# Linear attention and an MLP on one core: the first two units load in runs of eight tokens

## The chip, the cores and the metric

The kernel runs on one core of one Trainium2 chip. Its engines are TensorE (PE; its weight loads stand apart as PEld), VectorE (DVE), ScalarE (ACT), GpSimd (POOL) and SyncE (SP, which here only issues transfers). All run at the same time and wait for each other by semaphores. The metric is the device time of one execution in microseconds, lower is better; before the change it is 429.2 us, the median of three runs (428.32 to 429.36).

## The reference

Two blocks stand one behind the other. The first is a gated linear attention over 4 batches, 8 heads, 768 tokens and 48 numbers per head; the second a layer norm with an MLP from 384 to 1536 channels and back, and a residual.

```python
f = 1.0 / (1.0 + np.exp(-f_logit))
for t in range(S):
    state = f[:, :, t, :, None] * state + np.einsum('bhd,bhe->bhde', k[:, :, t], v[:, :, t])
    y[:, :, t] = np.einsum('bhd,bhde->bhe', q[:, :, t], state)
x = y.transpose(0, 2, 1, 3).reshape(B, S, H * D)
xn = (x - mu) / np.sqrt(var + 1e-06) * g_ln
return x + np.maximum(xn @ w_ch1, 0.0) @ w_ch2
```

## The kernel before

The 768 tokens are cut into 12 units of 64 tokens of all 4 batches, so that a unit has 256 rows: g = 0 holds batches 0 and 1, g = 1 batches 2 and 3, 128 rows each. Attention of a unit needs f, q and k with the 48 numbers of a head on the partitions and the tokens along the free axis, while DRAM holds 48 numbers of a token in a row. So each unit's f, q and k are loaded with tokens on the partitions and turned.

`load` (L495) issues, for f, q and k of units 0 to 2, one transfer per batch: 64 partitions (tokens) by 8 heads by 48 floats, each run 192 bytes long (96 KB, 512 runs). The heads stand 64 floats apart in the buffers `fraw`, `qraw` and `kraw`, whose last 16 columns of each head are set to zero once (L416). There is one such buffer each for f, q and k, so a unit's load has to wait until the unit before has been turned. `across` (L701) turns one half g of one of the three: four 128x128 transposes on TensorE (two heads at a time) into one bank of PSUM, from which ACT takes the sigmoid (f) or DVE the product with the gates (q, k). From unit 3 on (`DIRECT`), the turning is done by transfers through DRAM: ACT splits the numbers into planes of two bytes, a transfer writes them (L473), a transposing transfer brings them back (L492). These have one buffer `turned` in common for f and q, so that q of a unit must be used up before f of the next arrives.

Then come a scan over the gates from behind (`after`, L713) and from ahead (`upto`, L724), the scores (L811), the mask (`causal`), the values (L851), the state (L889), norm and turn (L930), and the MLP: first product L948 for unit 0, L1070 for unit 1, in blocks L999 from unit 2 on; second product L1080 for unit 0, L1099 later. The weights arrive as 64-bit numbers: twelve pieces are fetched (`f`), read by ACT (`r`), clipped by DVE (`c`) and written by ACT and POOL (`w`).

Nothing reorders the work: a string, `START`, lists it word by word for the first units, and a second one, `UNIT`, for every later unit. In it `a1.k` is stage k of the attention of unit 1, `a0.k0` the same for half 0 of unit 0, `l1f` loads f of unit 1 on SP (`L`: on ACT's queue), `h00` and `m1` are steps of the MLP, `p`, `P` and `x` the plane copies and the transposing transfers, and `d` a product of the identity with itself (L621) whose result nobody reads. Each engine's queue follows the order of the list. Another string, `BANKS`, says which of four PSUM banks each use takes.

Of the kernel before, what the change touches and what calls it, by code (L numbers as in the profile page):

```python
# [300 lines left out]


BANKS = """
012302310231021300132013021301230123012301230230232012120312121213201320132031202013201320312020
132013203120201320132031202013201320312020132013203120201320132031202013201320312020132013203120
30321032
"""

PLANES = """
# [1 line left out]
"""  # L311

START = """
a0.carried l0k0 L0f1 a0.gates0 l0q0 a0.kx0 d l0k1 l0q1 a0.gates1 f a0.after0 a0.k0 a0.upto0 L0v1
a0.q0 l0v0 a0.scores0 a0.causal0 r l1f a0.after1 f c a0.upto1 d w a0.q1 a0.kx1 a0.k1 l1k f
a0.values0 a0.stats0 l1q a1.gates r a0.scores1 a1.after c a0.kt a0.causal1 d d a1.kx a0.norm0 w
a0.turn0 a1.k r a1.upto a0.chunk c a0.state h00 a0.values1 f a1.kt a1.kept f w r a1.q h00 l2f
a1.carried l1v a1.scores f f a0.stats1 a0.norm1 a1.causal c r h00 l2q a0.turn1 c w a2.gates h01 w
a1.values r a1.stats f h01 f h01 c h00 a1.chunk w r a1.norm l3f c a1.state h01 a1.turn w r h01
a2.after r c w f h00 l2k a2.kept P3f0 m1 m1 r f c w m1 a2.upto f h01 h00 c w p3f1 m0 a2.kx l3k l2v  # L320
a2.k r c m1 x3f a2.q w m0 a2.carried l4f r a2.scores p3k1 c w u a2.causal P3k0 u U a2.kt l3q l3v
a3.gates m0 m0 u a2.values P3q1 a2.chunk t u m1 u x3k u a2.stats a2.state a3.after m1 P3q0 u m0 u
l4k a2.norm u P4f1 a2.turn a3.kept u u y2 x3q a3.k m0 a3.upto m1 U p4f0 m2 m2 m2 l5f p4k1 a3.q m2
x4f P4k0 T m1 l4q m2 m2 m2 m2 p5f0 p3K0 x4k s1 m2 p4q0 P3K1 a3.kt p4q1 t a3.carried a3.scores m2
m2 m2 L5k m1 a3.causal m2 a4.gates m1 m2 P5f1 a4.after m1 x4q m2 p5k0 a4.k m1 p5k1 m1 l4v s2
a4.upto l6f m2 a4.q m2 x5f a3.chunk a3.values m2 a3.stats m2 a3.state l5v a3.norm m2 m2 P4K1 p4K0
a3.turn l5q a4.kept m2 y3 a5.gates
"""
UNIT = """
a{n}.kt a{n}.carried p{p}f1 a{o}.after a{n}.scores m{m} a{n}.causal m{m} m{m} m{m} P{o}q0 m{m}  # L330
# [8 lines left out]
def kernel(  # L339
# [19 lines left out]
    nc = tc.nc  # L359
    B, H, S, D = q.shape  # L360
    P = 128
    T = 64
    G = B // 2
    NP = H // 2
# [14 lines left out]
    HALVED = 1  # L379
    PIECE = 768  # L380
    R = 2

    outer = ctx.enter_context(tc.tile_pool(name="outer", bufs=1))
    ident = outer.tile([P, P], FP32)
# [22 lines left out]
    def one_bank(name):  # L407
        return ps1.tile([P, 512], FP32, tag=f"one{next(banks_to_use)}", name=name)
# [4 lines left out]
    wide_heads = {}  # L413
    for name in "fqk":
        t = consts.tile([P, G, H, 64], FP32, name=f"{name}raw")
        nc.gpsimd.memset(t[:, :, :, D:64], 0.0)  # L416
        wide_heads[name] = t
    loaded = {}

# [7 lines left out]
    def raw_of(n, name):  # L427

        return wide_heads["k" if n >= DIRECT and name == "q" else name]
# [3 lines left out]
    def split(n, name, i, queue):  # L433
# [28 lines left out]
        if (n, name) not in halved:  # L462
# [4 lines left out]
        src = raw_of(n, name).rearrange("p g h e -> p (g h e)")[  # L467
            :, i * D:i * D + (H - 1) * R * D + 64]
        src = bass.AP(tensor=src.tensor, offset=src.offset,
                      ap=[src.ap[0], [R * D, H], [1, 64]]).bitcast(U16).rearrange(  # L470
                          "p h (c two) -> p two h c", two=2)
# [23 lines left out]
    def load(n, name, gs=range(B // 2), engines=(nc.sync,)):  # L495
        if n >= NU:
            return
        if name != "v":
            loaded[n, name] = raw_of(n, name)
        elif (n, name) not in loaded:  # L500
            loaded[n, name] = raws.tile([P, G, H, D], FP32, tag="rawv", name=f"v{n}")
        src = {"f": f_logit, "k": k, "q": q, "v": v}[name]
        for b in (b for b in range(B) if b // 2 in gs):
            to = loaded[n, name]
            if name == "v" or n < DIRECT:
                to = to[(b % 2) * T:(b % 2 + 1) * T, b // 2, :, 0:D]
                rows = src[b, :, n * T:(n + 1) * T, :].rearrange("h p d -> p h d")
            else:
                to = to.rearrange("p g h e -> p (g h e)")[
                    b * T // R:(b + 1) * T // R, 0:H * R * D].rearrange("p (h c) -> p h c", h=H)  # L510
                rows = src[b, :, n * T:(n + 1) * T, :].rearrange("h (p i) d -> p h (i d)", i=R)
            engines[b % len(engines)].dma_start(out=to, in_=rows)  # L512

    load(0, "f", (0,), (nc.sync, nc.scalar))

    power = consts.tile([P, 2], FP32)
    nc.vector.memset(power, -0.5)
# [162 lines left out]
    def attention(n):  # L680
# [6 lines left out]
        flat = "p s e -> p (s e)"  # L687
        at = {}

        def new(name, shape, **kw):  # L690
            if name not in at:
                at[name] = work.tile(shape, FP32, tag=name, name=f"{name}{n}", **kw)
            return at[name]

        def segments(gs):
            return slice(gs[0] * HS, (gs[-1] + 1) * HS)
# [1 line left out]
        def of(gs):  # L698
            return [ega for ega in enumerate(pairs) if ega[1][0] in gs]

        def across(src, g):  # L701

            pt = one_bank(f"tr{n}")
            for a in range(NP):
                nc.tensor.transpose(pt[:, a * P:(a + 1) * P],
                                    src[:, g, 2 * a:2 * a + 2].rearrange("p h e -> p (h e)"),
                                    ident)
            return pt.rearrange("p (s t) -> p s t", t=T)
# [19 lines left out]
        def times(dst, pts, by):  # L728
            for g, pt in pts.items():
                segs = segments([g])  # L730
                nc.vector.tensor_tensor(out=dst[:, segs], in0=pt, in1=by[:, segs, 1:E1],
                                        op=ALU.mult)

        def do_gates(gs=both):
            new("after", [P, NS, E1])
            new("upto", [P, NS, E1])
            if n >= DIRECT:
                nc.scalar.activation(out=gv[:, :, 1:E1], in_=turned["f"], func=AF.Sigmoid)
                return
            for g in gs:  # L740
                pt = across(loaded[n, "f"], g)
                nc.scalar.activation(out=gv[:, segments([g]), 1:E1], in_=pt, func=AF.Sigmoid)  # L742

        def do_after(gs=both):
# [4 lines left out]

        def do_k_across(gs=both):  # L750
            if n < DIRECT:
                at.setdefault("pk", {}).update((g, across(loaded[n, "k"], g)) for g in gs)

        def do_k(gs=both):
            kh = new("kh", [P, NS, T])
# [7 lines left out]
        def do_q(gs=both):  # L763
            qh = new("qh", [P, NS, T])
            if n < DIRECT:
                times(qh, {g: across(loaded[n, "q"], g) for g in gs}, at["upto"])
            else:
                nc.vector.tensor_tensor(out=qh, in0=turned["q"], in1=at["upto"][:, :, 1:E1],
                                        op=ALU.mult)
# [476 lines left out]
```

## Time and profile before

| what | before |
|---|---|
| median of three runs | 429.2 us (428.32 to 429.36) |
| span of the profiled execution | 427.6 us |
| PE busy, share of the span | 410.9 us, 96% |
| DVE / ACT / POOL busy | 329.3 / 227.1 / 120.1 us |
| DMA packets, bytes | 157663, 68.54 MB |

The profile has no total of its own beside the span; the median of the runs stands 1.6 us above it. Times in the trace count from the start of the span. The busy time of PE counts the whole stay of a product in the pipeline, so two products that follow each other overlap in it, and a busy PE isn't a PE at its peak. In the list of instructions over time a 4-byte product of 128 rows counts as two records and a transpose as one. PEclk is the granted clock of TensorE as a share of 2.4 GHz; until its first record it is written as 1.00.

### The profile page before, as it was taken

The page shows a single profiled execution, that of the slowest core. Times are in us where ns is not written, and L with a number is a line of the kernel's source. Part 1 is how long each engine was busy: PE and PEld are TensorE (multiplying, and loading weights), DVE is VectorE, ACT ScalarE, POOL GpSimd, SP SyncE. Part 2 cuts the span into 40 slices and gives each one's busy share as a digit, 9 for nine tenths or more (in the row PEclk, how much of TensorE's full clock was granted, in tenths as well). Part 3 has the DMA queues.
Part 4 walks back from the last instruction along what each step waited for, and adds up shares of the span by engine and source line. Part 5 has one row for each costly group of instructions (what it writes and reads, how often), then busy time and mean ns, then how long its engine had stood idle before and what let it go on. Part 6 is the DMA issues. An engine that isn't in the chain of part 4 may idle for free.

```text
span 427.6 us, 13031 instructions
## 1 busy us (share of the span) xinstructions
PE 410.9 (96%) x5509; PEld 391.7 (92%) x5509; DVE 329.3 (77%) x530; ACT 227.1 (53%) x380; POOL 120.1 (28%) x162
## 2 busy tenths in 40 slices
PE   4889999999999999999999989999999999999995
PEld 3769888779999999999999989999999999999995
DVE  5784866999797978878878868878878878664561
ACT  2579988446535574574574563573583451341320
POOL 2425536315224033033034024024025022022021
PEclk9899999999999999999999999999999999999998
DMA  9999998888999878879897869789977840100001
GB/s 133 239 224 264 207 239 197 212 181 204 217 226 174 205 161 208 191 164 201 171 197 182 201 131 209 181 191 196 174 173 166 181 89 10 31 2 18 20 11 34
DMA packets 157663, 68.54 MB, mean 160 GB/s; under 512 B 144976, under 2 KB 148240, under 8 KB 157600
## 3 DMA queue, kind: packets, MB, share of 16 engines
q1 hardware_dynamic: 144144, 52.94, 60.5%
q0 software_dynamic: 3648, 11.72, 8.0%
q10 hardware_dynamic: 9808, 3.00, 3.6%
q8 instruction: 45, 0.74, 0.7%
q14 instruction: 18, 0.15, 0.1%
HBM read 28.31 MB, written 22.02 MB: 118 GB/s over the span
## 4 chain that ended last, share of the span: by engine, by line
PE 90%; DMA 5%; SPq 2%; issue 1%; DVE 1%; ACT 1%; ACTq 0%
PE pp L1099 35%; PE bx L999 12%; PE by L999 11%; PE bz L999 4%; PE ph L1070 4%; PE po L1080 4%; PE ph L948 3%; PE py L851 3%; PE py L797 3%; DMA kraw<-in_k_dram 2%; PE bw L999 2%; PE shared L811 2%; PE bv L999 2%; PE shared L889 2%; PE xp L930 2%; SPq L512 2%
## 5 line engine op out<-in xcount | busy, mean ns | idle before, releaser
L1010 ACT ACTIVATE h<-h 128x512 f32<-128x512 f32 x50 | 31.5, 630 | 50.7 <-DVE h L1007 39.8
L1108 POOL TENSOR_TENSOR o<-p,x 128x192 f32<-128x192 f32 x44 | 32.8, 757 | 65.0 <-DVE p L1108 30.8
L1099 PE MATMUL pp<-mixed,h 128*128 128x192 f32 x264 | 46.5, 326 | 0.0
L1099 PE MATMUL pp<-mixed,s 128*128 128x192 f32 x264 | 45.0, 326 | 0.0
L1099 PE MATMUL pp<-w,h 128*128 128x192 f32 x264 | 44.9, 326 | 0.0
L1099 PEld LDWEIGHTS pp<-mixed,s 128*128 128x128 f32 x264 | 43.1, 190 | 0.1
L1099 PEld LDWEIGHTS pp<-w,h 128*128 128x128 f32 x264 | 42.8, 190 | 0.3
L1099 PEld LDWEIGHTS pp<-mixed,h 128*128 128x128 f32 x264 | 43.0, 190 | 0.0
L932 ACT ACTIVATE xt<-xp,gain 128x128 f32<-128x128 f32 x72 | 20.0, 375 | 40.5 <-PE xp L930 40.5
L1007 DVE TENSOR_TENSOR h<-h,bx 128x512 f32<-128x512 f32 x40 | 27.3, 683 | 15.8 <-PE bx L999 15.8
L999 PE MATMUL bx<-y,v 128*128 128x128 f32 x240 | 31.8, 275 | 0.0
L1108 DVE TENSOR_TENSOR o<-o,pp 128x192 f32<-128x192 f32 x55 | 18.9, 349 | 16.6 <-PE pp L1099 12.4
L713 DVE TENSOR_TENSOR_SCAN after<-gates,ends 128x1040 f32<-128x1040 f32 (+1 forms) x13 | 28.0, 2153 | 4.6 <-ACT gates L742 3.2
L999 PEld LDWEIGHTS bx<-y,v 128*128 128x128 f32 x240 | 29.2, 192 | 0.1
L724 DVE TENSOR_TENSOR_SCAN upto<-gates,starts 128x1040 f32<-128x1040 f32 (+1 forms) x13 | 28.1, 2161 | 0.4
L457 ACT COPY Kplanes<-kh 128x1024 uint16<-128x1024 uint16 x16 | 16.0, 1043 | 22.4 <-DVE kh L759 22.4
L877 POOL TENSOR_SCALAR rstd<-mv 128x2 f32<-128x2 f32 (+1 forms) x13 | 8.0, 615 | 70.3 <-DVE mv L875 70.2
L999 PE MATMUL by<-y,v 128*128 128x128 f32 x160 | 22.3, 281 | 1.1 <-issue 1.1
L1099 PE MATMUL pp<-w,s 128*128 128x192 f32 x132 | 23.3, 326 | 0.0
L1099 PEld LDWEIGHTS pp<-w,s 128*128 128x128 f32 x132 | 21.7, 190 | 0.0
L999 PE MATMUL bx<-y,w 128*128 128x128 f32 x160 | 21.7, 278 | 0.0
L1049 DVE TENSOR_TENSOR h<-by,h 128x512 f32<-128x512 f32 x10 | 6.9, 692 | 19.1 <-PE by L999 19.1
(162 smaller groups left out, 943.2 us busy)
## 6 DMA issues: line engine op xcount, KB each, us to landing
w_0words<-in_moe_w_ch_dram SPq DMA_DIRECT2D x7, 768.0 KB, 5.7
v<-in_v_dram SPq DMA_DIRECT2D x46, 96.0 KB, 3.8
kraw<-in_k_dram SPq DMA_DIRECT2D x44, 96.0 KB, 3.2
fhalves<-fplanes POOLq DMA_DIRECT2D x15, 256.0 KB, 3.6
out_dram<-o SPq DMA_DIRECT2D x40, 96.0 KB, 3.2
kraw<-in_q_dram SPq DMA_DIRECT2D x36, 96.0 KB, 3.6
Khalves<-Kplanes POOLq DMA_DIRECT2D x14, 192.0 KB, 3.5
khalves<-kplanes POOLq DMA_DIRECT2D x10, 256.0 KB, 3.4
```

The source lines that it names most:

```text
L457: nc.scalar.copy(out=planes[:, :, i], in_=src)
L713: nc.vector.tensor_tensor_scan(out=at["after"].rearrange(flat)[:, c0:c1][:, ::-1], data0=gt[:, c0 + 1:c1 + 1][:, ::-1], data1=ends.rearran ...
L724: nc.vector.tensor_tensor_scan(out=at["upto"].rearrange(flat)[:, c0:c1], data0=gt[:, c0:c1], data1=starts.rearrange(flat)[:, c0:c1], initi ...
L797: nc.tensor.matmul(py[half(b ^ r), r, e * D:(e + 1) * D], lhsT=qh[head_rows(r), 2 * e + b], rhs=kept[head_rows(r), b, e], start=e == 0, st ...
L932: nc.scalar.mul(out=xt[:, m, g * P:(g + 1) * P], in_=pt[:, m], mul=gain[:, m:m + 1])
L999: nc.tensor.matmul(banks[bank][:, i], lhsT=right[:, i * P:(i + 1) * P], rhs=left, start=new and i == 0, stop=True, skip_group_check=True)
L1007: nc.vector.tensor_tensor(out=out[to], in0=out[to], in1=bank, op=op)
L1010: nc.scalar.activation(out=out[to], in_=out[to] if bank is None else bank, func=AF.Relu)
L1070: nc.tensor.matmul(ph[:, j], lhsT=w1[:, m, (i + j) * P:(i + j + 1) * P], rhs=xt[:, m], start=m == 0, stop=m == KD - 1)
L1080: nc.tensor.matmul(po, lhsT=h[:, i, g * P:(g + 1) * P], rhs=w2[:, i], start=i == 0, stop=i == KF - 1)
L1099: nc.tensor.matmul(pp, lhsT=a[:, i], rhs=b[:, i], start=i == 0, stop=i == KH - 1)
L1108: engine.tensor_tensor(out=to, in0=x1, in1=x2, op=op)
```

## The change

Six loads (f, k and q of units 0 and 1) take another form. Now one transfer per half g brings eight tokens in a row: partition (b, h, o) holds the tokens 8o to 8o+7 of head h of batch b, 8 times 48 floats or 1536 bytes, 128 partitions, 192 KB. The buffers' free axis is then (token in the run j, number d), and turning needs the partitions split by head. `across` does this for these six with sixteen products per half in place of four transposes: for each of the eight tokens j of a run and each parity r of the head, the 48 columns of token j (and the 16 behind them) are the weights, and the 64 columns of the identity that belong to the heads of parity r move through. Parity 0 goes to the PSUM partitions 0 to 63, parity 1 to 64 to 127, so that a product uses 64 of the 128 columns of the array, and its 64 results lie eight floats apart. All other loads keep their form; the memset now clears what lies behind the 384 floats of a run, and the load of f half 1 goes whole to ACT's queue. `BANKS` and `START` have new texts; `UNIT`, `PLANES` and all other code are as before.

```diff
-a0.carried l0k0 L0f1 a0.gates0 l0q0 a0.kx0 d l0k1 l0q1 a0.gates1 f a0.after0 a0.k0 a0.upto0 L0v1
+a0.carried d L0f1 l0k0 a0.gates0 d a0.after0 a0.upto0 l0q0 a0.gates1 a0.kx0 a0.k0 a0.q0 a0.scores0
...
+    EIGHTS = "0f 0k 0q 1f 1k 1q".split()
+    OCT = 8
...
-        nc.gpsimd.memset(t[:, :, :, D:64], 0.0)
+        nc.gpsimd.memset(t[:, :, OCT * D // 64:], 0.0)
...
+        if f"{n}{name}" in EIGHTS:
+            rows = src.rearrange("(g b) h (o j) d -> g (b h) o (j d)", g=G, j=OCT)
+            for g in gs:
+                engines[g % len(engines)].dma_start(
+                    out=loaded[n, name][:, g, 0:OCT * D // 64].rearrange("p h e -> p (h e)"),
+                    in_=rows[g][:, n * T // OCT:(n + 1) * T // OCT])
+            return
...
-    load(0, "f", (0,), (nc.sync, nc.scalar))
+    load(0, "f", (0,))
...
+            if f"{n}{name}" in EIGHTS:
+                flat = src[:, g].rearrange("p h e -> p (h e)")
+                heads = ident.rearrange("p (e r o) -> p r e o", r=2, o=T // OCT)
+                for j in range(OCT):
+                    for r in range(2):
+                        to = pt[64 * r:64 * r + 64].rearrange(
+                            "p (a b o j) -> p j b a o", a=NP, b=2, j=OCT)[:, j]
+                        nc.tensor.matmul(to, lhsT=flat[:, j * D:j * D + 64], rhs=heads[:, r],
+                                         start=j == 0, stop=True, skip_group_check=True)
```

What the new list does to the engines is best seen where they start. On PE, at the head of the program, stood before (`tr` is the bank that a turned half goes to, `idle` the product `d`):

```order
L705 MATMUL tr_130<-ident,fraw 128x128 x4
L705 MATMUL tr_138<-ident,kraw 128x128 x4
L621 MATMUL idle<-ident 128x256
L705 MATMUL tr_149<-ident,fraw 128x128 x4
L705 MATMUL tr_167<-ident,qraw 128x128 x4
L811 MATMUL shared<-qh_166,kh_158 64x64 x16
L621 MATMUL idle<-ident 128x256
L705 MATMUL tr_214<-ident,qraw 128x128 x4
L705 MATMUL tr_220<-ident,kraw 128x128 x4
L851 MATMUL py_123<-v_163,sc_191 64x48 x16
```

And now:

```order
L631 MATMUL idle<-ident 128x256
L722 MATMUL tr_129<-ident,fraw 64x2x4x8 x16
L631 MATMUL idle<-ident 128x256
L722 MATMUL tr_154<-ident,fraw 64x2x4x8 x16
L722 MATMUL tr_172<-ident,kraw 64x2x4x8 x16
L722 MATMUL tr_192<-ident,qraw 64x2x4x8 x16
L832 MATMUL shared<-qh_191,kh_189 64x64 x16
L722 MATMUL tr_238<-ident,kraw 64x2x4x8 x16
L631 MATMUL idle<-ident 128x256
L872 MATMUL py_122<-v_230,sc_255 64x48 x16
```

A product that needs no load now stands ahead of the first turned half, and each half is sixteen products. On SP, which issues nearly all transfers, the same stretch read before:

```order
L512 DMA fraw<-in_f_logit_dram 64x8x48
L512 DMA kraw<-in_k_dram 64x8x48 x2
L512 DMA qraw<-in_q_dram 64x8x48 x2
L512 DMA kraw<-in_k_dram 64x8x48 x2
L512 DMA qraw<-in_q_dram 64x8x48 x2
L571 DMA w_0words<-in_moe_w_ch_dram 128x3x512
L512 DMA v_163<-in_v_dram 64x8x48 x2
L512 DMA fraw<-in_f_logit_dram 64x8x48 x4
L571 DMA w_256words<-in_moe_w_ch_dram 128x3x512
L512 DMA kraw<-in_k_dram 64x8x48 x4
```

And now:

```order
L509 DMA fraw<-in_f_logit_dram 128x1x384
L509 DMA kraw<-in_k_dram 128x1x384
L509 DMA qraw<-in_q_dram 128x1x384
L581 DMA w_0words<-in_moe_w_ch_dram 128x3x512
L509 DMA kraw<-in_k_dram 128x1x384
L522 DMA v_230<-in_v_dram 64x8x48 x2
L509 DMA qraw<-in_q_dram 128x1x384
L581 DMA w_256words<-in_moe_w_ch_dram 128x3x512
L509 DMA fraw<-in_f_logit_dram 128x1x384 x2
L509 DMA kraw<-in_k_dram 128x1x384 x2
```

The first two pieces of the weights (`w`) have moved up among the loads. Farther down SP's queue, where the last words of `START` stand, the transposing transfer of q of unit 4 came before the stores of unit 1's output (`out_dram<-o_1237`):

```order
L473 DMA fhalves_1329<-fplanes_1_1486 128x1024
L492 DMA_TRANSPOSE turned<-qhalves_1349 128x4x512
L1117 DMA out_dram<-o_1237 64x384 x4
L512 DMA v_1534<-in_v_dram 64x8x48 x4
L512 DMA fraw<-in_f_logit_dram 32x8x96 x4
L492 DMA_TRANSPOSE turned<-fhalves_1329 128x4x512
```

Now it comes behind them:

```order
L475 DMA fhalves_1557<-fplanes_1_1703 128x1024
L1138 DMA out_dram<-o_1358 64x384 x4
L494 DMA_TRANSPOSE turned<-qhalves_1580 128x4x512
L522 DMA fraw<-in_f_logit_dram 32x8x96 x4
L494 DMA_TRANSPOSE turned<-fhalves_1557 128x4x512
```

The load of v of unit 4 has moved ahead of this place, and f of unit 5 (the second `turned`) still comes behind q of unit 4.

## Rows read from the trace of the kernel before

**Rows 1.** The page: busy time by engine; PE's busy tenths in 40 slices.
```profile
PE 410.9 (96%) x5509; PEld 391.7 (92%) x5509; DVE 329.3 (77%) x530; ACT 227.1 (53%) x380; POOL 120.1 (28%) x162
...
PE   4889999999999999999999989999999999999995
```
**Rows 2.** PE over time: start, duration, line, tiles, records, idle time before and releaser.
```profile
4.69 1.09 PE L705 MATMUL tr<-ident,fraw 128*128 128x128 f32 x4 [4.69 <-DMA fraw<-in_f_logit_dram]
...
17.03 0.63 PE L705 MATMUL tr<-ident,fraw 128*128 128x128 f32 x4 [1.01 <-DMA fraw<-in_f_logit_dram]
...
51.78 7.93 PE L1070 MATMUL ph<-xt,w 128*128 128x256 f32 x36
```
**Rows 3.** PE's waits, 0 to 60 us: total, times, longest.
```profile
PE tr L705 <- DMA fraw<-in_f_logit_dram: 6.1, 3, 4.7
PE tr L705 <- DMA kraw<-in_k_dram: 1.4, 2, 0.9
PE shared L889 <- issue: 0.9, 1, 0.9
PE ph L948 <- ACT kt L842: 0.8, 1, 0.8
PE shared L811 <- DVE qh L731: 0.8, 1, 0.8
...
PE tr L705 <- ACT h L950: 0.2, 1, 0.2
```
**Rows 4.** The chain of waits, 0 to 130 us: start, length, line, records.
```profile
51.95 7.77 PE ph L1070 x36
59.72 2.68 PE ph L948 x24
...
64.98 0.87 PE tr L705 x8
...
71.90 1.08 PE py L797 x64
72.98 0.95 PE shared L811 x64
73.92 1.03 PE kp L840 x8
...
80.11 1.08 PE py L851 x64
81.19 0.72 PE shared L889 x64
...
89.87 0.66 PE xp L930 x6
...
107.13 1.09 PE bx L999 x8
108.22 0.89 PE bz L999 x8
```
**Rows 5.** Busy time of the engines in one microsecond, then granted clock, DMA share, GB/s.
```profile
20.00:21.00 1.00, 1.00 (x7) 1.00 (x6) 1.00 (x1) 0.52 (x1) 1.00 (x1) 0.50 1.60 175
```
**Rows 6.** Transfers issued in 0 to 60 us: size and time to landing.
```profile
fhalves<-fplanes SPq DMA_DIRECT2D x1, 256.0 KB, 2.5
```
**Rows 7.** SP, ACT and PE over time, around unit 3's first block product.
```profile
119.28 2.09 SPq L492 DMA_TRANSPOSE turned<-qhalves  x1
121.63 2.41 SPq L1117 DMA_DIRECT2D out_dram<-o  x4
...
130.45 2.13 SPq L492 DMA_TRANSPOSE turned<-fhalves  x1
...
138.01 1.09 ACT L738 ACTIVATE gates<-turned 128x1024 f32<-128x1024 f32 x1
...
140.69 1.16 PE L999 MATMUL bw<-y,w 128*128 128x128 f32 x8
```
**Rows 8.** The tile `turned`, 90 to 170 us: its transfers.
```profile
DMA to landing us min/median/max: 5.0/5.4/6.7
```

More of the change, by code (lines that the diff above doesn't have):

```diff
@@ L303 @@
 BANKS = """
-012302310231021300132013021301230123012301230230232012120312121213201320132031202013201320312020
-132013203120201320132031202013201320312020132013203120201320132031202013201320312020132013203120
-30321032
+012301230132012301230123012301230123012301230123012310310312020210321032103210323201320132013232
+103210321032320132013201323210321032103232013201320132321032103210323201320132013232103210321013
+23210321
 """
@@ L313 @@
 START = """
-a0.carried l0k0 L0f1 a0.gates0 l0q0 a0.kx0 d l0k1 l0q1 a0.gates1 f a0.after0 a0.k0 a0.upto0 L0v1
[L315 to L325, printed above, removed]
@@ L326 @@
-a4.upto l6f m2 a4.q m2 x5f a3.chunk a3.values m2 a3.stats m2 a3.state l5v a3.norm m2 m2 P4K1 p4K0
-a3.turn l5q a4.kept m2 y3 a5.gates
+a0.carried d L0f1 l0k0 a0.gates0 d a0.after0 a0.upto0 l0q0 a0.gates1 a0.kx0 a0.k0 a0.q0 a0.scores0
+f l0k1 a0.after1 l0v0 l0q1 r a0.kx1 a0.causal0 d L0v1 c a0.upto1 a0.k1 f l1f l1k w f a0.values0 r
+a0.q1 a1.gates a0.scores1 d a0.stats0 l1q c a0.kt w a0.causal1 a1.after a0.norm0 a1.kx f a1.k
+a1.upto a0.chunk l2f r a0.turn0 c a0.values1 a0.state a1.kt w h00 h00 f a1.kept r a0.stats1 a1.q c
@@ new lines @@
+a2.gates a0.norm1 a1.carried l1v a1.scores f w a0.turn1 h00 a1.causal r l2k f c h01 w a1.values
+a1.chunk h01 a1.stats f r h00 l3f h01 c f w h00 a1.norm a2.after a1.turn r c h01 h01 w r l2q f f
+m1 P3f0 a2.kx p3f1 m1 a2.upto a2.k r c c w h00 m1 a2.q a1.state l3k f w l2v r m1 c r a2.kept w x3f
+a2.kt c w m1 a2.carried r p3k1 a2.scores m0 a2.causal c a2.chunk P3k0 t w l3q l4v a2.values h01
+a2.state a2.stats u u m0 a3.gates l4f P3q1 U a3.after a2.norm m0 P3q0 u x3k u u m0 a2.turn u m1
+l4k u y2 P4f1 m0 x3q a3.kept u u p4f0 m1 a3.k l3v m2 a3.upto u u U p3K0 l5f m0 m1 a3.q m2 m2 P3K1
@@ L328 @@
+s1 m2 a3.carried a3.scores x4f a3.causal p4k1 m2 a3.kt P4k0 m2 m2 m2 T l4q t m2 p5f0 m2 a4.gates
+m2 m2 p4q0 a4.after m1 m2 p4q1 L5k a3.values a3.chunk m2 x4k a4.upto a3.state a4.k m2 m1 P5f1 m1
+a3.stats m1 m1 P4K1 m2 s2 p5k0 a3.norm p5k1 m2 x4q p4K0 a4.kept m2 a3.turn a4.q m2 l6f x5f y3 l5q
+m2 a5.gates m2 l5v m2
 """
@@ L699, in of, with across @@
             return [ega for ega in enumerate(pairs) if ega[1][0] in gs]
-        def across(src, g):
+        def across(name, g):
             pt = one_bank(f"tr{n}")
+            src = loaded[n, name]
+            if f"{n}{name}" in EIGHTS:
[7 more added lines that the diff above has]
+                                         start=j == 0, stop=True, skip_group_check=True)
+                return pt.rearrange("p (s t) -> p s t", t=T)
             for a in range(NP):
@@ L740, in do_gates @@
             for g in gs:
-                pt = across(loaded[n, "f"], g)
+                pt = across("f", g)
                 nc.scalar.activation(out=gv[:, segments([g]), 1:E1], in_=pt, func=AF.Sigmoid)
@@ L751, in do_k_across @@
             if n < DIRECT:
-                at.setdefault("pk", {}).update((g, across(loaded[n, "k"], g)) for g in gs)
+                at.setdefault("pk", {}).update((g, across("k", g)) for g in gs)
         def do_k(gs=both):
@@ L765, in do_q @@
             if n < DIRECT:
-                times(qh, {g: across(loaded[n, "q"], g) for g in gs}, at["upto"])
+                times(qh, {g: across("q", g) for g in gs}, at["upto"])
             else:
```

## The prediction, on record before the result

> **What bounds the kernel now.** I read the page first, then the list of PE over time from its start, PE's waits in the first 60 us, and the chain of waits for the price of each kind of product. The page shows a kernel that TensorE bounds: 96% busy, with tenths below 9 only in the first three slices, in one slice past the middle and in the last [rows 1]. After the start PE has nothing to wait for worth naming, so a change to the start moves the end by as much as it moves the moment at which a fixed piece of PE's work is done. I take as that moment the first product of unit 1's MLP, at 51.78 us [rows 2]: in both lists the same work lies ahead of it on PE, apart from how halves are turned.
>
> **What those 51.78 us hold.** Prices at full clock come from the chain [rows 4]. A turned half (four transposes) is 0.87 / 2 = 0.435 us; the four `d` are one 256-column product each, 7.77 / 18 = 0.43; scores of a unit 0.95, values 1.08, state 0.72, carried 1.08; three norm transposes 0.33; one step of the first MLP 2.68 / 2 = 1.34. Ahead of the moment stand 14 turned halves (6.09), 4 `d` (1.73), scores of two units (1.90), values of two (2.16), four groups of `kp` at 0.435 like the other transposes (1.74), state of two (1.44), four groups of norm transposes (1.32), ten MLP steps (13.40) and one carried (1.08): 30.9 us. So 20.9 us of the 51.78 are lost. Of these the waits explain 10.6: 6.1 for f, 1.4 for k, 0.9 that nothing explains, 0.8 twice, and three of 0.2 of which the last is shown [rows 3].
>
> A second loss is changing between products on the whole array and products on quarters of it. Eight transposes take 1.03 right after scores and 0.87 elsewhere, four products 1.09 right after scores and 0.89 next to it: 0.16 to 0.20, say 0.18, per change [rows 4]. PE's list has 16 changes ahead of the moment, 2.9 us. The rest, 20.9 - 10.6 - 2.9 = 7.4, is half clock and short waits that busy time hides: the first four transposes take 1.09 us, the same four at 17.03 0.63 [rows 2], which are the levels of 1.2 and 2.4 GHz, and at 20 to 21 us the granted clock is 0.50 again, 1.2 GHz [rows 5].
>
> **What the change adds.** Twelve halves (three names, two units, two halves) are turned by sixteen products of 64 columns on half the array. The trace has no such form. The nearest row is the scores: 32 products of 64 columns with 64 weight columns, on four quarters side by side, in 0.95 us, so eight per quarter [rows 4]. Sixteen products on two halves are eight per half too, so 0.95 if the two halves run side by side as the quarters do. Bounds: 0.72, the state's row, as short as any such group; 1.08, the values' row; and 1.78 if the two halves of the array don't overlap, since each product is then half of a 128-column one, 0.89 / 4 / 2 = 0.111. I take 0.95, whose columns match, which adds 12 x (0.95 - 0.435) = 6.2 us. The new form is one more kind to change to: 21 changes in place of 16, 5 x 0.18 = 0.9. The list of PE's work until the moment is then 30.9 + 6.2 = 37.1 us and its changes 3.8.
>
> **What it takes away.** The six loads of units 0 and 1 become twelve transfers of 192 KB in place of twenty-four of 96 KB, with runs of 1536 bytes in place of 192. The nearest transfer with long runs is one of 256 KB from SP, which lands 2.5 us after its issue, in the same crowd [rows 6]. So f half 0, issued by 1 us, lands at about 3.5 in place of 4.69 [rows 2]; it can't come later than before with less in front of it. One `d` now stands ahead of it, 0.43 x 2 = 0.9 at half clock, so PE idles 3.5 - 0.9 = 2.6 us where it idled 4.7. The other waits for f and k (6.1 - 4.7 + 1.4 = 2.8) go: their transfers have half the SP issues and far fewer runs ahead of them. What is late next is DVE and ACT: the 0.8 for `qh` stays, since q is turned behind k and f as before; of the 1.4 for ACT I keep half, because the pieces of the weights now arrive earlier and spread ACT's work; the unexplained 0.9 stays. Waits: 2.6 + 0.8 + 0.7 + 0.9 = 5.0, where they were 10.6.
>
> Half clock: PE then works from 3.5 us on with hardly a gap, since turning takes longer than the loads. The clock should rise well ahead of the 17 us by which it had, and the second fall around 20 us should go. I halve the 7.4 to 3.7; bounds are 1.5 (it rises at once, and what remains is the work ahead of it) and 7.4 (as before).
>
> **The sum.** 37.1 of work, 5.0 of waits, 3.8 of changes, 3.7 of half clock and hidden waits: 49.6 in place of 51.78, 2.2 us earlier. Nothing behind it is new work for PE, so the span falls from 427.6 to 425.4; the runs' median stands 1.6 above the span, hence 427.0. Not counted because hidden: the ACT and POOL rows, whose work is the same; the memset, of the same size; `BANKS`, which can only add waits for a bank, and four banks serve about as many uses.
>
> **The rivals.** *No overlap of the halves of the array.* A half then costs 1.78, 12 x 0.83 = 10 us more than forecast; waits of some 3 us would vanish under it: 427.0 + 7 = 434.0. For it: every product of the new form uses all rows. Against it: quarters overlap in the scores' row, where two of four share their rows. The Trainium skill, TensorE: Matmul & The Clock Gate, Part 3 (The mechanism, What overlaps and what doesn't), says that a weight load overlaps running products only when it goes to another row group. By that rule all new loads would be exposed, and the time would be this rival's; here the trace disagrees: with all rows in use two products of 128 columns take 0.445 and one of 256 columns 0.43, so the second weight load costs next to nothing [rows 4].
>
> *The clock stays low.* PE gains gaps because `qh` and the mask pace it, and 1.2 GHz holds as long as before: 7.4 in place of 3.7, 430.7. For it: the clock did fall again around 20 us [rows 5]. Against: fewer gaps.
>
> *The clock rises at once, and the waits go.* 1.5 in place of 3.7 and ACT's 0.7 gone: 427.0 - 2.9 = 424.1. For it: from 3.5 us on PE has products one behind the other, where before it waited 10.6 us. Against: the row at 20 us shows a fall with the engine busy all through [rows 5].
>
> *A wait later on takes the gain.* q of unit 4 is transposed by a transfer issued at 119.28, ahead of unit 1's stores (2.41 us from 121.63) [rows 7]; now behind them, some 5 us later. It lands 5.0 to 6.7 us after issue [rows 8]; DVE must use it before f of unit 5 can come into the same buffer, which took from 130.45 to 138.01 [rows 7]. So the gates start near 139 at the latest bound, while PE's first block product comes 2 us earlier than 140.69; ACT's gates and copies stand between. Slack was some 2 us, and 1.5 could be lost: 428.5.
>
> *The loads land no earlier,* because the weights' pieces have moved up in front of them: 2.8 of waits and 1.2 at the head return, 431.0.
>
> **Chances.** Forecast 0.36 (its own range 425.8 to 428.4), clock at once 0.22, late wait 0.18, clock low 0.13, no overlap 0.07, loads no earlier 0.04. About 0.3%, 1.3 us, is what a measurement of this kernel can tell from no change. Below 427.9: 0.30 of the forecast's, all 0.22, 0.03 of the late wait: 0.55. Above 430.5: half and more of the clock's (0.07), no overlap (0.07), most of the loads' (0.04): 0.18. Between: 0.27. The range of 8 in 10 leaves out no overlap, part of the loads' and a tail below: 423.6 to 430.9.
>
> **What would show it.** The first turned half should start near 3.5 us and one at full clock take about 0.95, sixteen products together; 1.8 there means no overlap. PE's waits for f and k should shrink to the head. Granted clock should show no 0.50 around 20 us. The first product of unit 1's MLP should start near 49.6, and the first block product of unit 3 two us earlier than 140.69; if the first holds and the second doesn't, the late wait has it. I am wrong if that product of unit 1 starts behind 51.78.

## The result, and the profile after

The changed kernel takes 432.9 us, median of four runs (431.98 to 435.46), against 429.3 for the kernel before beside it: a ratio of 1.0124 (95% interval 1.0088 to 1.0159), 1.2% slower. I had forecast 427.0 within 423.6 to 430.9. The profiled execution has a span of 430.7 us where before had 427.6.

The page of the changed kernel, busy time and PE's tenths, as in [rows 1]:

```profile
PE 416.2 (97%) x5845; PEld 398.0 (92%) x5845; DVE 328.2 (76%) x530; ACT 227.3 (53%) x380; POOL 124.3 (29%) x162
...
PE   7779999999999999999999999999999999999995
```

PE has 336 MATMUL and 336 LDWEIGHTS more, 672 instructions. PE over time after the change (start, duration, line, tiles, records, idle time before it and what ended it), as in [rows 2]:

```profile
4.32 1.97 PE L722 MATMUL tr<-ident,fraw 128*64 128x64 f32 x32 [0.93 <-DMA fraw<-in_f_logit_dram]
...
10.75 1.10 PE L722 MATMUL tr<-ident,qraw 128*64 128x64 f32 x32
...
14.98 0.56 PE L872 MATMUL py<-v,sc 64*64 64x48 f32 x23
17.13 0.34 PE L872 MATMUL py<-v,sc 64*64 64x48 f32 x9 [1.60 <-issue]
...
54.62 2.76 PE L1091 MATMUL ph<-xt,w 128*128 128x256 f32 x12
...
145.40 1.16 PE L1020 MATMUL bw<-y,w 128*128 128x128 f32 x8
```

The first product of unit 1's MLP, the prediction's moment, starts at 54.62, where [rows 2] has 51.78 and I had 49.6; unit 3's first block product at 145.40, where [rows 7] has 140.69. PE's waits of the first 60 us (total, times, longest), as in [rows 3]:

```profile
PE idle L631 <- POOL ident masks.py:199: 2.2, 1, 2.2
PE py L872 <- issue: 1.8, 2, 1.6
PE shared L832 <- issue: 1.5, 2, 1.3
PE shared L910 <- issue: 1.2, 1, 1.2
PE tr L722 <- DMA fraw<-in_f_logit_dram: 0.9, 1, 0.9
PE shared L832 <- DVE qh L752: 0.8, 1, 0.8
```

The loads' waits are gone but for 0.9; in their place stands "issue", 4.6 us in the chain (1.60, 1.33, 1.21, 0.20 and 0.23), where [rows 3] has 0.9. It is the stall that the profile gives no cause for, and it comes in the middle of groups whose operands had long been there: 23 of 32 records of the values run, then PE stands for 1.6 us. The chain also has the price of a turned half at full clock:

```profile
22.46 1.33 issue
...
25.74 2.02 PE tr L722 x64
...
28.42 1.21 issue
```

Two halves in 2.02: 1.01 each. What the stalls have in common shows when PE's instructions between them are counted. Rows of stretches that begin and end at a stall (start to end, length, then busy time and, in brackets, number for PE and PEld; at the end granted clock, DMA share, GB/s):

```profile
17.13:23.78 6.65, 5.33 (x127) 5.07 (x126) 2.57 (x6) 4.01 (x7) 2.62 (x3) 0.74 1.02 263
23.79:29.61 5.82, 4.62 (x126) 4.10 (x126) 5.30 (x7) 3.65 (x5) 2.29 (x2) 1.00 0.88 136
29.62:44.95 15.33, 14.90 (x379) 13.82 (x380) 9.59 (x14) 12.05 (x25) 6.63 (x5) 1.00 0.72 157
44.96:79.92 34.96, 33.99 (x507) 30.42 (x507) 23.94 (x35) 33.00 (x52) 19.71 (x13) 1.00 0.94 227
79.93:107.82 27.89, 27.40 (x254) 21.47 (x254) 27.19 (x44) 13.57 (x22) 8.18 (x9) 1.00 0.92 187
```

MATMUL and LDWEIGHTS together make 253, 252, 759, 1014 and 508; these rows leave out PE's few other instructions (73 for semaphores in all), which the trace holds too: counted with them it is 256, 256, 768, 1024 and 512. Every stall falls on a border of 256 instructions. The kernel before has the same: its two stalls, the one of [rows 3] at 46.6 us and one of 1.1 at 251.9, stand 22 blocks apart. First PE's wait there (of the whole span), then the stretch between the two:

```profile
PE by L999 <- issue: 1.1, 1, 1.1
```

```profile
46.60:251.93 205.33, 204.19 (x2803) 192.48 (x2802) 170.59 (x262) 123.87 (x197) 63.49 (x81) 1.00 0.85 196
```

2803 + 2802 = 5605, and with the others 5632 = 22 x 256. The same count in all 19 traces of this case finds 61 stalls named "issue" behind PE's first product, of 0.2 to 4.2 us, and 60 of them at one and the same place of a block of 256 (the other has 0.4 us, in `unit1`). Shortly before each stall ends, the profile's queue of instructions moves 16 KB. Around the first stall of the changed kernel (all packets from 10.43 to 14.40 us, then the same from 14.40 to 15.80):

```profile
DMA packets 656, 1.09 MB, mean 276 GB/s; under 512 B 74, under 2 KB 277, under 8 KB 656
...
DMA packets 493, 0.36 MB, mean 256 GB/s; under 512 B 304, under 2 KB 489, under 8 KB 492
...
q8 instruction: 1, 0.02, 5.6%
```

Counted back from the stall's end, PE ran the first instruction of that block at 10.43. The 16 KB of the next block start 4.0 us after it, last 1.25, and PE goes on 1.4 us after their end. At all seven stalls of this execution that last figure is 1.2 to 1.4.

This is the theory that I tested, S (supply): a block of 256 PE instructions is fetched only when the one before has begun, and PE stalls where it gets through a block sooner than the next is there. "Only when" is too strong: the trace has one packet of 16 KB for each block, and later in the execution some of them start earlier than that (at 123.39, 3.0 us before PE ran the first instruction of the block before). The Trainium skill, Runtime: NRT & Kernel Launch, section Instruction fetch mechanics, says that an engine's instructions come in blocks of 16 KiB (256 of them), and that crossing a border is mostly hidden; the trace agrees with the size, and on the hiding at 39 of the changed kernel's 46 borders; at the other seven it differs, with 0.2 to 1.6 us each. The rival, P (price), was that the work itself costs it: 12 halves at 0.58 more, the clock, and stalls that belong to the places where they stand.

### The profile page after: what moved, and what is told of

Read it like the earlier page. It is cut to its first block, busy times and chain, and to the rows that moved or that the text cites. A ratio compares the mean times of both kernels' runs of the same rounds, so it can differ in the third digit from the quotient of the medians.

```text
span 430.7 us, 13687 instructions
## 1 busy us (share of the span) xinstructions
PE 416.2 (97%) x5845; PEld 398.0 (92%) x5845; DVE 328.2 (76%) x530; ACT 227.3 (53%) x380; POOL 124.3 (29%) x162
## 4 chain that ended last, share of the span: by engine, by line
PE 96%; issue 1%; DMA 1%; DVE 0%
PE pp L1120 35%; PE bx L1020 13%; PE by L1020 11%; PE bz L1020 4%; PE ph L969 4%; PE tr L722 4%; PE po L1101 4%; PE ph L1091 4%; PE py L872 3%; PE shared L832 3%; PE py L818 3%; PE bw L1020 2%; PE bv L1020 2%; PE shared L910 2%; PE xp L951 2%
## 5 line engine op out<-in xcount | busy, mean ns | idle before, releaser
L734 DVE TENSOR_TENSOR_SCAN after<-gates,ends 128x1040 f32<-128x1040 f32 (+1 forms) x13 | 29.0, 2234 | 6.7 <-ACT gates L763 3.7
L475 POOL DMA_DIRECT2D qhalves<-qplanes x9 | 4.9, 548 | 62.0 <-ACT qplanes L474 61.8
L474 ACT COPY qplanes<-kraw 128x1024 uint16<-128x1024 uint16 x18 | 18.6, 1038 | 6.2 <-DMA kraw<-in_q_dram 6.2
```

Source lines behind the costliest of these rows:

```text
L474: nc.scalar.copy(out=planes.rearrange("p two (h c) -> p two h c", h=H), in_=src)
L734: nc.vector.tensor_tensor_scan(out=at["after"].rearrange(flat)[:, c0:c1][:, ::-1], data0=gt[:, c0 + 1:c1 + 1][:, ::-1], data1=ends.rearran ...
```

## The experiments

**The change in two: the list, and the form.** `list_only` keeps the new `START` and `BANKS` and turns everything in the old form; `form_only` puts the new form under the old list.

```diff
# list_only, on the changed kernel (and the old memset)
-    EIGHTS = "0f 0k 0q 1f 1k 1q".split()
+    EIGHTS = []
# form_only: the changed kernel with START and BANKS of before
```

> The new list and banks, but all six loads and turnings in the old form (the memset too). Theory S (supply): PE's instructions reach it in blocks of 256, in the start a block can begin no sooner than about 6 us after the one before, and the 672 instructions that the new turning adds make the stalls named issue. Then without them at most one such stall over 0.5 us stands ahead of unit 1's MLP, waits for f, k and q come back (4 to 6 us), the clock as before: first product of unit 1's MLP at 49 to 52 us, time 427 to 430, at least 3 us under the changed kernel. Theory P (price): the 12 halves cost 0.58 us more each at full clock and twice that at half, and the stalls belong to the new list (its order or its banks). Then three or four stalls of 1.2 to 1.6 us remain here, and with the loads' waits back the time is 431 to 434.

> The old list and banks with the new loads and turning of all six. S: the same 672 instructions are added, so three or four stalls of 1 to 1.6 us come up, 256 instructions apart, though the list is the old one; loads' waits shrink: 430 to 433. P: the stalls stay away, as in the kernel before (one of 0.9): waits of about 7 us go, 7 of work come: 428 to 430.

`list_only`: 431.2 us, ratio 1.0076 (1.0017 to 1.0135); `form_only`: 429.6, 1.0026 (0.9974 to 1.0078). The first is not what S gave (427 to 430), and lies where P had it: the list alone costs. Its stalls did go, as S says and P doesn't: one of 0.4 us is left ahead of unit 1's MLP, which starts at 51.83, but it waits for f:

```profile
PE tr L726 <- DMA fraw<-in_f_logit_dram: 5.7, 2, 3.3
PE idle L631 <- POOL ident masks.py:199: 2.2, 1, 2.2
...
PE ph L969 <- issue: 0.4, 1, 0.4
```

`form_only` has stalls again, under the old list and at other work (waits of the first 60 us):

```profile
PE tr L722 <- DMA fraw<-in_f_logit_dram: 4.4, 1, 4.4
PE xp L951 <- DVE xn L940: 1.4, 1, 1.4
PE shared L832 <- issue: 1.4, 2, 0.9
PE ph L969 <- issue: 1.0, 1, 1.0
```

2.4 us of them up to unit 1's MLP, where before has 0.9: the form brings stalls there, as S says, and the new list makes 4.6 of them. But the time again lies where P had it (428 to 430). And over the whole execution the stalls come to 2.4 us in `form_only` and 2.3 in `list_only`, where the kernel before has 2.1 and the changed kernel 6.1: neither half of the change adds much by itself.

**One unit alone**, under the new list and (unit 0) under the old.

```diff
-    EIGHTS = "0f 0k 0q 1f 1k 1q".split()
+    EIGHTS = "0f 0k 0q".split()          # unit0, old_unit0; unit1: "1f 1k 1q"
```

> The new list, unit 0 alone in the new form (six halves, 336 instructions fewer than the changed kernel), unit 1 in the old one. S: the stalls at 15.5 us and at about 22.5 us stay, since the instructions ahead of them are nearly the same, the one near 28.4 goes or halves; 1.5 to 3 us under the changed kernel, 430 to 431.5. P: half of the price goes, 6 x 0.58 = 3.5 us, stalls as in the changed kernel, waits for unit 1's loads come back by 1 to 2: 430.5 to 432.

> The new list, unit 1 alone in the new form, unit 0 in the old one. S: 336 instructions fewer before 20 us, so the stall at 15.5 us goes and at most two of over 1 us are left, both later; waits for unit 0's loads come back (3 to 5 us): 429 to 432. P: stalls stand where the changed kernel has them, in unit 0's values and unit 1's scores: 431 to 434.

> The old list and banks, unit 0 alone in the new form. S: 336 instructions fewer than the old list with all six in the new form (429.6): its stall near 19.7 us goes or moves, head as there (f at 4.4 us): 427 to 430. P: 6 x 0.58 = 3.5 us less work than there, loads' waits of unit 1 back (about 2): 427 to 429.

`unit0` 432.6 (ratio 1.0103, 1.0044 to 1.0162) and `unit1` 433.8 (1.0146, 1.0072 to 1.0219): both lie above what S gave, and `unit1` where P had it. In `unit0` the stalls ahead of unit 1's MLP still come to 4.6 us (2.3, 0.9 and 1.4); the first is at the same place, the others at borders further on. `unit1` has only one big one, 2.1 us, later as S says, and waits of 2.8 and 2.3 for f beside it. Half of the form under this list costs as much as all. `old_unit0`: 428.3, ratio 0.9999 (0.9972 to 1.0026), with no such stall listed among the waits ahead of unit 1's MLP.

**Moving the borders.** `shift64` puts 64 instructions that nobody needs ahead of the changed kernel's first product.

```diff
+        for i in range(0 if idled else 16):
+            nc.tensor.matmul(pi[0:32, 2 * P:2 * P + 4], lhsT=ident[:, 0:32], rhs=ident[:, 0:4],
+                             start=True, stop=True)
```

> The changed kernel with 16 tiny products (32 x 4, nobody reads them), 32 records and 64 instructions, ahead of the first idle product, where PE waits for f anyhow. S: every block's border lies 64 instructions earlier in the work: the first stall comes in the middle of k half 1 of unit 0's turning (16 records into it) in place of the values, the second in f half 1 of unit 1's turning in place of the scores, the third in unit 1's k turning in place of the state; by count, MATMUL and LDWEIGHTS between two stalls still make 256. P, or any cause that lies in the work itself: the stalls stay in the values, the scores and the state.

A single execution, span 433.6. PE over time:

```profile
13.15 1.03 PE L729 MATMUL tr<-ident,kraw 128*64 128x64 f32 x26
16.64 0.69 PE L729 MATMUL tr<-ident,kraw 128*64 128x64 f32 x6 [2.46 <-issue]
```

The stall left the values for k half 1 of unit 0, as S asks, 26 records into it (I had written 16, a miscount: of the 32 records by which the border moved, 23 are values and 2 the `d`, which leaves 7 at the end of k's 32, so 25). The second and third did not come where I put them: the next block's 16 KB started 1.3 us after its predecessor had begun, in place of 4.0, and were in time. A border is where a stall can be; whether it comes depends on the fetch.

`before_nop148`, `before_nop88` and `list_nop144` shift borders with empty instructions ahead of all else.

```diff
+    for _ in range(148):        # 88, 144
+        nc.tensor.nop(hint="pad", nofuse=True)
```

> The kernel before with 148 empty instructions (NoOp) in PE's queue ahead of all else, where PE waits 4.7 us for f anyhow: every border between two blocks of 256 instructions lies 148 instructions earlier in the work, nothing else changes. S: by the trace of before, counting the time of each 256 instructions and asking 5.8 us before 60 us and 3.4 behind, stalls of 1.1 us in all are left where the same count gives 3.7 for the kernel before (2.9 by its trace): 1 to 2.5 us faster than before, both of its stalls (0.9 at 46 us, 1.1 at 250 us) gone. P, or any cause in the work itself: the stalls stay where they are, and the time within 0.3%, or slower if PE is late at the head.

> The same with 88 empty instructions. S: by the same count this is the worst place of the borders, 7.7 us of stalls in place of 3.7 (2.9 at 36 us, 1.4 at 106, 0.9 at 126, 1.2 at 185, 1.3 at 281): 2 to 5 us slower than before, with stalls at those places. P: within 0.3%, stalls at 46 and 250 us as before.

> The new list with the old form of all loads (431.2 us, 0.8% over before) and 144 empty instructions ahead. S: the count gives 2.6 us of stalls in place of 8.4 (its trace showed 3.2): 2 to 4 us under the same kernel without them, so 427 to 429.5. P: as without them, 430 to 432.

437.6 (ratio 1.0196, 1.0146 to 1.0246), 429.9 (1.0058, 1.0024 to 1.0091) and 436.7 (1.0172, 1.0123 to 1.0221). The first and the third were to be faster and are slower, for a reason that I had not reckoned with: an empty instruction takes 0.07 us (PE's first product starts at 11.78 us after 148 of them and at 7.44 after 88, 60 in 4.34), so the head is late. Their stalls aren't as counted either: 1.7 and 1.2 us at 42.9 and 50.6 us in `before_nop148`, where the count left 1.1 in all. `before_nop88` is slower by as much as S gave, but its stalls come to 2.0 us, about the 2.1 of the kernel before, where the count had 7.7: its time speaks for neither theory. (What the expectations name as shown by the traces, 2.9 for the kernel before and 3.2 for `list_only`, is 2.1 and 2.3 in their waits.) The borders moved all the same. Of PE's waits in `before_nop88`, and PE over time:

```profile
PE tr L707 <- issue: 7.4, 1, 7.4
...
PE bx L1001 <- issue: 1.2, 1, 1.2
PE ph L950 <- issue: 0.8, 1, 0.8
```

```profile
37.23 0.60 PE L950 MATMUL ph<-xt,w 128*128 128x128 f32 x4 [0.82 <-issue]
```

The stalls of before at 46 and 250 us are gone from the work that had them, and the new ones end at 37.2 and 107.8 us, two of the five places forecast; the other three did not stall. So the place of a stall goes with the count of instructions and not with the work, and its length is not foretold by such a count.

**The price of the products, by itself.** `quads` orders a run's partitions by parity, so that a product uses 64 rows and the two parities lie in opposite quarters (which also makes two transfers of each load); `old_quads` is that under the old list; `eight_wide` makes eight products per half with 128 weight columns, half the instructions, and turns the even heads alone (the odd heads get other numbers); `old_eight_wide` the same under the old list.

```diff
# quads (its loads are two transfers of 64 partitions)
+                        nc.tensor.matmul(to, lhsT=flat[own, j * D:j * D + 64], rhs=ident[own, own],
# eight_wide
+                    nc.tensor.matmul(to, lhsT=flat[:, j * D:j * D + P], rhs=heads[:, 0],
```

> The changed kernel, but with the partitions of a run ordered by the head's parity first: a product of the turning then uses 64 rows and 64 columns, the two parities lie in opposite quarters of the array and can run side by side (and each load is two transfers of 64 partitions). Same number of instructions. S: a turned half alone gets faster, about 0.5 us at full clock in place of 1.01, but its 64 instructions stay, so blocks of 256 instructions are entered as far apart as before (5.8 to 6.7 us in the first 30 us), the stalls grow by what the products save, and unit 1's MLP starts at 53 to 55 us: 430.5 to 433.5. P: 12 x 0.5 = 6 us go from PE's work and from the end: 425 to 428.

> The list and banks of before with the turning on opposite quarters. S: as the old list with the new form (429.6), perhaps 1 us less where no block holds PE up: 428.5 to 430. P: 6 us less than that: 423 to 425.

> The changed kernel with eight products per half in place of sixteen: each has 128 weight columns and 64 columns of the identity, so the even heads alone are turned and the rows of the odd heads get other numbers; everything else runs as in the changed kernel. Half the instructions of the turning (384 fewer), about the same time on PE: 16 records of 64 columns, at 0.055 to 0.065 us 0.9 to 1.05 us per half at full clock, where the changed kernel has 1.01. S: the stalls ahead of unit 1's MLP fall from 4.6 us to under 2, its first product starts at 50 to 52.5 us (54.6 in the changed kernel) and the time is 2 to 4 us under the changed kernel's 432.9. P (the price of a half is what costs): within 1 us of the changed kernel.

> The list and banks of before with the eight wide products per half (odd heads get other numbers, as above). S: the form's time on PE without its extra instructions, on the list whose first borders cost least: stalls ahead of unit 1's MLP under 1.2 us (2.4 with sixteen products), 427 to 429. P: as the old list with sixteen products, 429.6 within 0.7.

`quads` 437.5 (ratio 1.0251, 1.0206 to 1.0295), `old_quads` 431.6 (1.0101, 1.0066 to 1.0136), `eight_wide` 453.5 (1.0592, 1.056 to 1.0625), `old_eight_wide` 448.2 (1.0468, 1.0446 to 1.0489). My prices were wrong in all four, so they don't tell S from P; why `quads` is that much slower stays open. In `quads` a half of 64 rows is no cheaper, 61 records in 2.02 us; in `eight_wide` a product with 128 weight columns costs far more than one with 64, two halves 3.68 at full clock:

```profile
26.50 2.02 PE L723 MATMUL tr<-ident,kraw 64*64 64x64 f32 x61
```

```profile
55.49 3.68 PE L720 MATMUL tr<-ident,qraw 128*128 128x64 f32 x32
```

That is 0.115 us a record against 0.032. In `eight_wide`, whose blocks last 10 us and more up to 60 us, no stall is left in that stretch (its one stall, 1.6 us, ends at 68.7); but its work is 0.83 a half dearer, 10 us in twelve at full clock, and its first ten halves cost twice their price there (the first 3.68 us for 16 records), which is half clock by that price: the trace has no granted clock before 52.9 us.

`burst` runs 512 records (1024 instructions) behind the first units' list and again behind the last product.

> The changed kernel with 256 products of 64 x 64 by 64 columns (512 records, 1024 instructions, nobody reads the result) behind the first units' list, among the loads, and the same again behind the last product, where hardly a transfer runs. At the rate of the scores (64 records in 0.95 us) a burst takes 7.6 us. S: stalls in both, 256 instructions apart; a block every 3.5 to 4 us at the end (14 to 16 us for the burst), every 4 to 6.5 us in the middle. P: no stalls, 7.6 to 10 us for each.

```profile
143.14 12.11 PE L1218 MATMUL burst<-ident 64*64 64x64 f32 x406
156.03 3.30 PE L1218 MATMUL burst<-ident 64*64 64x64 f32 x105 [0.79 <-issue]
...
442.35 15.15 PE L1218 MATMUL burst<-ident 64*64 64x64 f32 x512
```

At 0.029 us a record from start to start a block lasts 3.7 us, and where hardly a transfer runs it has no stall, though S had put some there; among the loads it has one of 0.8. A burst is not the 7.6 us that I had reckoned from the scores, which use four quarters. So where it is quiet the fetch keeps up with a block in 3.7 us, and the end shows no floor.

Up to the first burst `burst` is the changed kernel's work in another execution. Its stalls up to unit 1's MLP are 0.6, 2.5, 0.7 and 0.7 us, at four of the same five borders, and that MLP starts at 52.82: the places stay, the lengths don't.

**Why a block is late.** `one_piece` loads one piece of the weights of each shape and uses it for all (it leaves the other pieces out): the same instructions on PE, fewer transfers. `late_two` only moves two pieces back in the list.

```diff
# one_piece
+        if (r, w) not in first:
+            first[r, w] = stage.tile([P, r, 2 * w], I32, tag="words", name=f"{name}words")
+            nc.sync.dma_start(out=first[r, w], in_=src.bitcast(I32))
# late_two, in START
-f l0k1 a0.after1 l0v0 l0q1 r a0.kx1 a0.causal0 d L0v1 c a0.upto1 a0.k1 f l1f l1k w f a0.values0 r
+l0k1 a0.after1 l0v0 l0q1 f a0.kx1 a0.causal0 d L0v1 a0.upto1 r a0.k1 l1f f c l1k w f a0.values0 r
```

> The changed kernel with one piece of the weights fetched for each shape and used for all pieces of that shape (the other weights are not loaded, so the MLP has wrong weights); some ten transfers of 768 KB fewer among the first loads, the same instructions on PE. What it tells apart is why a block takes 5.8 to 6.7 us in the start and 3.1 to 3.7 later. S with the transfers as cause (a block's 16 KB wait behind other packets): the 16 KB start 1 to 2 us after the block before begins in place of 3 to 4, stalls ahead of unit 1's MLP fall from 4.6 to under 2.5 us, 2 to 4 us under the changed kernel. S with a fixed price of a block: starts and stalls as in the changed kernel, time within 1 us of it.

> The changed kernel with the first two pieces of the weights fetched later in its list, behind q of unit 0 and behind the first half load of f of unit 1 (and read and clipped so much later); every other word as it was, PE's instructions the same. S with transfers as cause: the 16 KB for the blocks begun at 10.4 and 17.1 us start 1.5 to 3 us after them in place of 4.0, the first two stalls (1.6 and 1.3 us) lose half, and the time is 1 to 3 us under the changed kernel's 432.9, 430 to 432. If the crowd is the same whatever the order: stalls and time as in the changed kernel.

`one_piece`: 427.3, ratio 0.9995 (0.998 to 1.0011), 5.6 under the changed kernel's 432.9, more than the 2 to 4 that S gave with transfers as cause. `late_two`: 433.2, 1.0124 (1.0095 to 1.0152), the changed kernel's own ratio. `one_piece` over time, its stalls (it has no others), and the moment, which is 5.35 us earlier than in the changed kernel:

```profile
15.03 0.33 PE L874 MATMUL py<-v,sc 64*64 64x48 f32 x9 [0.23 <-issue]
...
19.69 0.44 PE L834 MATMUL shared<-qh,kh 48*64 48x64 f32 x10 [0.87 <-issue]
...
34.74 0.80 PE L834 MATMUL shared<-qh,kh 48*64 48x64 f32 x36 [0.45 <-issue]
...
49.27 2.76 PE L1093 MATMUL ph<-xt,w 128*128 128x256 f32 x12
```

Same instructions, same first border (23 values before it), 1.55 us of stalls in place of 4.6; the 16 KB start 3.3, 2.0 and 2.2 us after their predecessor block in place of 4.0, 4.0 and 3.0. So other transfers make the fetch late. The stalls are 3.0 of the 5.35 us; most of the rest is the clock, which rises sooner here and doesn't fall again. From 16 to 20 us its granted clock is 1.00 (the third figure from the end), where the changed kernel's is 0.68:

```profile
16.00:20.00 4.00, 3.13 (x112) 2.92 (x108) 2.38 (x6) 3.23 (x6) 2.51 (x3) 1.00 0.60 143
```

`late_two` shows that moving two of them back does not help:

```profile
17.68 0.57 PE L832 MATMUL shared<-qh,kh 48*64 48x64 f32 x22
22.41 0.69 PE L832 MATMUL shared<-qh,kh 48*64 48x64 f32 x10 [4.16 <-issue]
```

The first stall goes, and the second, at the same border as in the changed kernel, is 4.16 us: its 16 KB start 5.5 us after the block before. What was won at one border was lost at the next.

**What is worth keeping.** `old_fk0`: the old list, f and k of unit 0 alone in the new form, 224 instructions more than before.

> The list and banks of before with f and k of unit 0 alone in the new form (four halves, 224 instructions more than before). Unit 0's six halves on this list gave 428.3, 1.0 of before. S: fewer instructions ahead of 20 us, the head's gain (f 0.3 us earlier) and k's wait gone, 1 to 1.5 us against 4 x 0.58 = 2.3 us of work, half of it at half clock: within 0.4% of before, and a time below both kernels only if borders fall well.

426.7 us, ratio 0.9966 (0.9945 to 0.9986): 0.3% faster than the kernel before. That is little, and it is the best of a dozen kernels tried, so part of it may be chance. Its stalls in the whole execution come to 0.3 us. Its waits in the first 60 us:

```profile
PE tr L723 <- DMA fraw<-in_f_logit_dram: 4.3, 1, 4.3
PE tr L727 <- DMA fraw<-in_f_logit_dram: 1.3, 1, 1.3
...
PE shared L911 <- issue: 0.3, 1, 0.3
```

Under the old list the ratio goes 0.9966, 0.9999, 1.0026 with 224, 336 and 672 instructions added; their intervals overlap from one to the next.

## Why the prediction was wrong

**The step that failed is one term of the waits: "the unexplained 0.9 stays".** I carried the row that I could not explain [rows 3] into the sum as a constant, and it is the one term that grows with the instructions which the change adds. It measured 4.6 us up to the moment, 3.7 more than forecast: PE waits for its own instructions there. The premise that behind the start PE has nothing to wait for missed the same thing: the kernel before has a stall of 1.1 at 250 us, and in the changed kernel two further stalls, 0.98 at 78.9 and 0.50 at 107.3 us, stand between the moment and unit 3's first block product. What is shown is where the stalls stand, and by `one_piece` that other transfers lengthen them. Their lengths I couldn't forecast, and most of S's times were missed (those of `list_only`, `form_only` and `unit1` fell in P's ranges). The rest of the ledger of the moment, 54.62 against 49.6:

- A turned half: 0.95 forecast, 1.01 measured, 12 x 0.06 = 0.7 more. The bounds held. No overlap of the array's halves (1.78) is refuted for this form. By the Trainium skill, TensorE: Matmul & The Clock Gate, Part 3 (The mechanism, What overlaps and what doesn't), a weight load overlaps running products only when it goes to another row group (the section also names a background weight buffer); the trace disagrees with the first for this form, since all rows are in use and a half takes 1.01. In `eight_wide`, where all columns are in use too, a product took 0.23 (two records of 0.115), twice that rival's 0.111; that would fit the rule, but no row tells what part of it is weight loads.
- The head: 2.6 us of idle forecast, 2.17 and 0.93 measured, 0.5 more. The 192 KB landed at 4.27 in place of 3.5; the 256 KB of [rows 6] were too quick a model for a transfer among many.
- Waits for f and k: gone but for the head, as forecast. The 0.8 for `qh` stayed, as forecast; of the 0.7 for ACT nothing was left.
- Half clock: 3.7 forecast. The first three halves and the `d` between them took about 2.9 us more than at full clock (starts at 4.32, 6.22, 7.37, 9.14 and 10.75 in the trace, 1.0 a half and 0.55 for `d` at full clock). The second fall did not go, it came at 17.5 us, behind the stall of 1.6 us, and lasted 3.4 us at 0.50, 1.2 GHz, worth 1.7. Together 4.6, 0.9 more, though `burst` shows the same work without a second fall:

```profile
18.00:20.00 2.00, 2.00 (x43) 2.00 (x41) 0.59 (x1) 1.96 (x4) 0.38 (x1) 0.50 1.06 290
```

Stalls 3.7, halves 0.7, head 0.5, half clock 0.9, ACT -0.7: 5.1, and the miss is 5.0. It closes that well by luck: the 3.8 for changes was never measured, and the `d` ahead of the first half also ran slow.

Behind the moment I was wrong by the same cause. Unit 3's first block product is 4.7 us late: 2.84 at the moment, 1.5 in the two further stalls, 0.4 in other places. At 250 us the kernel before loses 1.1 us at a border of its own and the changed kernel has none there, which gives some of it back: the last product starts 3.1 us later than before. The late wait for q of unit 4 did not decide: ACT's gates start at 144.53, later than forecast, and the block product at 145.40 follows the scores without a gap:

```profile
144.53 1.06 ACT L759 ACTIVATE gates<-turned 128x1024 f32<-128x1024 f32 x1 [7.52 <-DMA turned<-fhalves]
```

"The clock stays low" came near in time (430.7 forecast as a median) and not in mechanism.

Open: which words of the new list make its stalls longer than the old list's with the same form (4.6 against 2.4 us), and why the list alone costs 0.8%, though its stalls in all are those of before; its profiled execution, with a span of 428.6, shows 1.0 us of it. The lengths depend on when each 16 KB get through, which differs between executions, as `burst` shows. The spread of the runs doesn't show it: the changed kernel's four lie within 3.5 us, and those of the kernel before within 1.3 beside it, but within 5.6 beside `list_only`.

## What to carry to other kernels

A row "issue" in PE's waits is to be explained before it is carried into a sum: count PE's instructions between two of them; where that was a multiple of 256, as at all but one here, PE was waiting for its own instructions. Short products are then not priced by their time alone: among heavy loads the blocks of 256 came 5.8 to 6.7 us apart in the changed kernel, however soon PE was through. There is no fixed price to add: blocks of 3.7 us cost nothing at the end of `burst`, and one of the changed kernel from 221.3 us on lasted 2.4 with no stall behind it, its successor's 16 KB having started 0.4 us before it. A change that splits a product into many may be worth trying on its few most urgent users first: `old_fk0` is the only one here with the right numbers that came out ahead, by little.

## What the runs showed of the hardware that I had not expected

- Three blocks of 256 PE instructions began 5.8 to 6.7 us after the one before in the first 30 us of the changed kernel, each after a stall (4.7 to 5.8 in `one_piece`, with fewer transfers); 3.7 us a block runs without a stall where hardly a transfer is (`burst`).
- At each of the 60 stalls on a border of 256 PE goes on 1.2 to 1.8 us after a packet of 16 KB on its instruction queue has ended.
- A 4-byte record with 64 moving columns takes 0.115 us with 128 weight columns and 0.032 with 64, when two such lie on different columns of the array; 64 rows in place of 128 change nothing (`quads`).
- An empty instruction in PE's queue takes 0.07 us (60 more of them put off PE's first product by 4.34 us).
